# Two subtractions of the filter on VectorE instead of GpSimd

## The chip, the core and the metric

The kernel runs on one core of one Trainium2 chip. A core has TensorE (PE, with its weight load PEld), VectorE (DVE), ScalarE (ACT), GpSimd (POOL) and SyncE (SP), which issues DMAs; each works through its own instructions in order. The metric is the device time of one execution in microseconds. Before the change: 3201.36 us, the median of 3 runs (3199.89 to 3202.30).

## The reference, cut to what matters

Three parts follow one another. The change lies in the first, a filter in the frequency domain over 4 batches of 3072 rows of 256 columns:

```python
X = np.fft.rfft(x, axis=1)
Yr = Xr @ w_r - Xi @ w_i + b_r
Yi = Xr @ w_i + Xi @ w_r + b_i
Yr = np.sign(Yr) * np.maximum(np.abs(Yr) - lam, 0.0)   # the same for Yi
y = np.fft.irfft(Yr + 1j * Yi, n=3072, axis=1)
```

The second part makes u and v from relu(y @ w_in), normalises v over its columns, mixes it over all 3072 rows with w_spatial, adds a bias, multiplies by u and by w_out. The third is relu(x @ w_in) squared, scaled, and multiplied by another w_out. All data are float32.

## The kernel before

Every product is made in split precision: an operand is written as a high part (a copy in a type of fewer bits, fp32r) and a low part (the operand minus the high part), and two or three matmuls of the parts are added in PSUM. So each operand that comes from memory needs a copy (high) and a subtraction (low) before TensorE can use it.

The filter is a Fourier transform in two factors, 3072 = 96 x 32, and back. Its pieces, by function:

- `s1`: 96-point transform of x; one call takes a tile of two columns of the 96 x 32 grid. 16 calls a batch. The result `ps_z` goes through `z_sb` to the scratch tensor `zd`.
- `g_stage`: 32-point transform of t (what `zd` holds, read in another order) into `ps_g`, of which there is one buffer (`pg` has one). It is evacuated as `xh` (ScalarE, L375, L376), `xt` and `xl` (VectorE, L379, L380) and a negated copy (ScalarE, L383).
- `mix`: the products with w_r and w_i into `ps_m`, then the threshold: `ma`, `mt` (VectorE, L424, L425), `yh` (ScalarE, L426), `yl` (VectorE, L427).
- `g2_stage`: 32-point transform back into `ps_v`, evacuated by ScalarE (`v_sb`, L444) to the scratch tensor `vd`.
- `s3`: 96-point transform back of v (what `vd` holds) into `ps_y`, two buffers, each freed by a VectorE addition into `y_sb` (L469). Four calls make one chunk `y_hl` (L478, L482).
- `v_product`: of the second part, v = relu(y @ w_in) into `ps_vp`, its statistics (`bn`, `mv`) and, for three tiles at a time, a chain of small VectorE operations on 128 x 3 numbers (`rs`, L595 to L603) whose end releases the normalising L607 on ScalarE and L609 on VectorE.

The order of the work is written out by hand. The loop over k (L629 to L676) has 50 steps; each makes one `g_stage(k)`, one `mix(k - 1)`, one `g2_stage(k - 2)` and, spread over the step so that the counts come out, calls of `s1`, `s3` and `v_product`. The evacuations are not issued where their product is: each goes into a list of stages (`ch`), of which every further call issues one. After the loop a tail (L688 to L698) runs what is left of `s3` and `v_product`, while the first loads of the mixing are issued. x is done in the first 300 us; v is needed from about 144 us on.

`Stream` (L259) handles the three operands from memory: `xs` (tile `x_f`, both parts in one tile `x_hl`, 96 x 512), `ts` (`t_f`, `t_h`, `t_l`, 128 x 1024) and `vs` (`v_f`, `v_hi`, `v_lo`, 96 x 512). `load` issues the DMA, `make` the copy (L294, L296) and the subtraction (L298). `steady` is false until step k = 1, that is while the pipeline is filled; from then on the copies are ScalarE's. All three streams have `lo_on = "pool"`. GpSimd also issues the DMAs of the constants (`cg`, `cv`, L527) and of the normalised v (`vn`, L614).

Of the kernel before, what the change touches and what calls it, by code (L numbers as in the profile page):

```python
# [34 lines left out]
def f(ap):  # L35
    return ap.bitcast(F32)
# [191 lines left out]
def attention(tc, nc, x, w_r, w_i, b_r, b_i, c_f, c_b, c_g, c_v, c_s, zd, vd, yd, vn, chunks, cd, follow, nb=NB):  # L228
# [28 lines left out]
    steady = [False]  # L257

    class Stream:  # L259
# [25 lines left out]
        def make(self, n):  # L285
            while self.split < min(n, self.total):
                i = self.split
                self.load(i + 1)
                if self.loaded == i:
                    break  # L290
                raw = self.t[i]
                hi, lo = self.parts()
                if self.hi_on == "act" or steady[0] or i % 2 == 1:
                    nc.scalar.copy(hi, raw)  # L294
                else:
                    nc.vector.tensor_copy(hi, raw)  # L296
                on_pool = self.lo_on == "pool" and steady[0]
                (nc.gpsimd if on_pool else nc.vector).tensor_sub(lo, raw, f(hi))  # L298
                self.t[i] = (hi, lo)
                self.t.pop(i - self.bufs, None)  # L300
                self.split += 1
# [923 lines left out]
```

## Time and profile before

| | us |
|---|---|
| median of 3 timed runs | 3201.36 |
| the profiled execution, its own time | 3198.43 |
| its span in the trace | 3196.7 |
| TensorE busy (matmul) | 3085.7 (97%) |
| VectorE busy | 2309.5 (72%) |
| ScalarE busy | 1428.3 (45%) |
| GpSimd busy | 392.8 (12%) |

The filter takes the span up to about 556 us; the rest is the mixing and the output. Shares are of the whole span; the filter's own are in the rows below, by stretch. Busy time counts a stalled instruction as busy. Releasers of a wait are inferred. The granted clock is TensorE's, as a share of full speed (1.00 is 2.4 GHz, 0.50 is 1.2 GHz).

### The profile page before, as it was taken

Reading aid. Unit: us, or ns where it says so; the run is one execution under the profiler, and the core shown is the slowest. Engines: PE = TensorE matmul, PEld = TensorE weight load, DVE = VectorE, ACT = ScalarE, POOL = GpSimd, SP = SyncE. Lnnn points to the kernel's source line nnn. Section 1 sums busy time; section 2 is a strip of 40 time slices with the busy share of each in tenths; the row PEclk is TensorE's granted clock in tenths of the full one; section 3 lists DMA queues with packets and bytes.
Section 4 is the critical chain, followed back from the end, with each engine's and each line's share of the span. In section 5 each row is a group of like instructions: output and inputs, shape, how many; then the busy total and the mean of one; then the engine's idle time right before and its main releaser. Section 6 shows DMA issues by size and latency. Waiting matters only on the chain.

```text
span 3196.7 us, 46508 instructions
## 1 busy us (share of the span) xinstructions
PE 3085.7 (97%) x17960; PEld 3012.8 (94%) x17960; DVE 2309.5 (72%) x3495; ACT 1428.3 (45%) x2244; POOL 392.8 (12%) x497
## 2 busy tenths in 40 slices
PE   6989998999999999999999999999999999999999
PEld 5888986999999999999999989999999999999999
DVE  5877988787878888888878755656566656656564
ACT  5776766433434333434434334444444444444443
POOL 2665544021000210000000100000000000000000
PEclk7999999999999999999999999999999999999999
DMA  8987659487456956466471621111111111110210
GB/s 245 291 263 228 228 184 322 162 314 288 159 198 200 359 212 233 148 217 246 158 238 44 239 82 55 48 50 65 55 65 55 65 55 65 55 64 29 70 45 15
DMA packets 230517, 488.30 MB, mean 153 GB/s; under 512 B 22356, under 2 KB 116376, under 8 KB 230296
## 3 DMA queue, kind: packets, MB, share of 16 engines
q1 hardware_dynamic: 197224, 353.51, 33.4%
q0 software_dynamic: 33072, 131.82, 11.2%
q8 instruction: 140, 2.29, 0.3%
q14 instruction: 81, 0.66, 0.1%
HBM read 322.72 MB, written 162.53 MB: 152 GB/s over the span
## 4 chain that ended last, share of the span: by engine, by line
PE 76%; DVE 13%; DMA 5%; ACT 3%; issue 2%; POOL 0%; SPq 0%; ACTq 0%; DVEq 0%; POOLq 0%
PE acc L856 28%; PE ps_h L1066 17%; PE oacc L1087 17%; PE ps_o L1047 4%; PE ps_u L1029 4%; PE ps_m L413 3%; PE ps_vp L578 2%; DMA st_a<-in_moe_w_spatial_dram 2%; DVE a_hl L837 1%; DVE kept L873 1%; DMA st_b<-vn 1%; DVE b_hl L837 1%; DMA st_b<-t 1%; PE ps_g L366 1%; DVE bn L591 1%
## 5 line engine op out<-in xcount | busy, mean ns | idle before, releaser
L856 PE MATMUL acc<-a_hl,b_hl 128*128 128x384 f32 x7056 | 1239.5, 336 | 32.7 <-DVE kept L873 13.3
L856 PEld LDWEIGHTS acc<-a_hl,b_hl 128*128 128x128 f32 x7056 | 1232.9, 189 | 39.3 <-ACT kept L877 13.0
L1066 PE MATMUL ps_h<-x_hl,w 128*128 128x384 f32 x3072 | 580.8, 337 | 1.5 <-ACT x_hl L1050 0.9
L1087 PE MATMUL oacc<-q_hl,w 128*128 128x384 f32 x3072 | 575.4, 336 | 0.6 <-DVE q_hl L1073 0.6
L1066 PEld LDWEIGHTS ps_h<-x_hl,w 128*128 128x128 f32 x3072 | 543.3, 188 | 2.1 <-ACT x_hl L1050 1.3
L1087 PEld LDWEIGHTS oacc<-q_hl,w 128*128 128x128 f32 x3072 | 537.0, 188 | 0.9 <-DVE q_hl L1073 0.8
L833 ACT CAST a_hl<-a 128x768 fp32r<-128x768 f32 x253 | 211.7, 837 | 524.1 <-PE acc L856 436.7
L1073 DVE TENSOR_TENSOR q_hl<-r,q_hl 128x768 fp32r<-128x768 f32 x256 | 245.4, 959 | 230.7 <-ACT q_hl L1072 230.7
L1071 DVE TENSOR_TENSOR r<-r 128x768 f32<-128x768 f32 x256 | 244.8, 956 | 204.4 <-ACT r L1070 204.4
L1072 ACT CAST q_hl<-r 128x768 fp32r<-128x768 f32 x256 | 213.7, 835 | 301.8 <-DVE r L1071 301.8
L1070 ACT ACTIVATE r<-ps_h 128x768 f32<-128x768 f32 x256 | 208.3, 814 | 310.6 <-PE ps_h L1066 307.2
L837 DVE TENSOR_TENSOR a_hl<-a,a_hl 128x768 fp32r<-128x768 f32 x253 | 241.4, 954 | 137.5 <-ACT a_hl L833 137.0
L837 DVE TENSOR_TENSOR b_hl<-b,b_hl 128x512 fp32r<-128x512 f32 x295 | 202.0, 685 | 0.0
L833 ACT CAST b_hl<-b 128x512 fp32r<-128x512 f32 x295 | 181.8, 616 | 0.0
L578 PE MATMUL ps_vp<-win,y_hl 128*128 128x512 f32 x576 | 154.5, 404 | 18.3 <-ACT v_sb L444 15.0
L874 POOL DMA_DIRECT2D md<-kept x112 | 60.7, 542 | 828.4 <-DVE kept L873 824.0
L1029 PE MATMUL ps_u<-y_hl,w 128*128 128x384 f32 x768 | 145.7, 339 | 1.8 <-DVE y_hl L1015 1.8
L1047 PE MATMUL ps_o<-g,w 128*128 128x384 f32 x768 | 139.2, 337 | 1.6 <-DVE g L1037 1.0
L578 PEld LDWEIGHTS ps_vp<-win,y_hl 128*128 128x128 f32 x576 | 102.1, 190 | 40.4 <-ACT v_sb L444 16.8
L1029 PEld LDWEIGHTS ps_u<-y_hl,w 128*128 128x128 f32 x768 | 135.5, 190 | 3.1 <-DVE y_hl L1015 2.1
L1047 PEld LDWEIGHTS ps_o<-g,w 128*128 128x128 f32 x768 | 133.4, 188 | 2.6 <-DVE g L1037 1.6
L873 DVE TENSOR_TENSOR kept<-acc,kept 128x768 f32<-128x768 f32 x112 | 102.9, 952 | 22.1 <-PE acc L856 21.1
(139 smaller groups left out, 3700.7 us busy)
## 6 DMA issues: line engine op xcount, KB each, us to landing
a<-in_moe_w_spatial_dram SPq DMA_DIRECT2D x144, 384.0 KB, 5.0
b<-vn SPq DMA_DIRECT2D x168, 256.0 KB, 5.3
md<-kept POOLq DMA_DIRECT2D x112, 384.0 KB, 5.3
m<-md SPq DMA_DIRECT2D x56, 768.0 KB, 5.6
st_a<-in_moe_w_spatial_dram SPq DMA_DIRECT2D x72, 384.0 KB, 6.4
vn<-vr POOLq DMA_DIRECT2D x96, 256.0 KB, 4.0
s<-a POOLq DMA_DIRECT2D x48, 384.0 KB, 5.8
x_f<-in_x_dram SPq DMA_DIRECT2D x32, 384.0 KB, 6.5
```

What stands on the lines that cost most here:

```text
L578: nc.tensor.matmul(ps, y[:, a, k, o:o + 128], win[k][:, w, :], start=c == 0, stop=c == 5)
L833: nc.scalar.copy(s[:, 0, :], t)
L837: sub(s[:, 1, :], term.pop((kind, n)), f(s)[:, 0, :])
L856: nc.tensor.matmul(acc[d][:, h, 0:TH], b[:, m, d * 128:(d + 1) * 128], a[:, w, h * TH:(h + 1) * TH], start=fresh and i == 0 and c == 0, st ...
L1029: nc.tensor.matmul(ps[:, d, 0:TH], win[k][:, a, o:o + 128], y[:, w, k, :], start=c == 0, stop=c == 5)
L1047: nc.tensor.matmul(ps[:, h, 0:TH], wo[k // 2][:, a, o:o + 128], g[:, w, k, :], start=c == 0, stop=c == 11)
L1066: nc.tensor.matmul(ps[:, e, 0:TH], w[:, a, o:o + 128], x[:, i, j, :], start=c == 0, stop=c == 5)
L1070: nc.scalar.activation(r, ps[:, :, 0:TH], AF.Relu)
L1071: nc.vector.tensor_mul(r, r, r)
L1072: nc.scalar.copy(s[:, 0], r)
L1073: nc.vector.tensor_sub(s[:, 1], r, f(s)[:, 0])
L1087: nc.tensor.matmul(ps[:, h, 0:TH], w[:, a, o:o + 128], s[:, i, e, :], start=ff == 0 and c == 0, stop=ff == 2 * NP - 1 and c == 2)
```

## The change

One condition in `Stream.make`: GpSimd is chosen for the subtraction only if the stream is the one of t.

```diff
                 else:
                     nc.vector.tensor_copy(hi, raw)
-                on_pool = self.lo_on == "pool" and steady[0]
+                on_pool = self.lo_on == "pool" and steady[0] and self.tag == "t"
                 (nc.gpsimd if on_pool else nc.vector).tensor_sub(lo, raw, f(hi))
```

The subtractions of x and v go to VectorE's queue at the place where `make` is called. On VectorE, in a step of the loop in which two tiles of x are made and none of v (the first stretch), before the change:

```order
L424 TENSOR_SCALAR ma<-ps_m 128x512
L425 TENSOR_TENSOR mt<-ps_m,ma 128x512
L427 TENSOR_TENSOR yl<-mt,yh 128x512
L379 TENSOR_TENSOR xt<-ps_g,xh 128x512
L380 TENSOR_TENSOR xl<-ps_g,xt 128x4x128
```

On VectorE, the same step with the change:

```order
L424 TENSOR_SCALAR ma<-ps_m 128x512
L425 TENSOR_TENSOR mt<-ps_m,ma 128x512
L298 TENSOR_TENSOR x_hl<-x_f,x_hl 96x512
L427 TENSOR_TENSOR yl<-mt,yh 128x512
L298 TENSOR_TENSOR x_hl<-x_f,x_hl 96x512
L379 TENSOR_TENSOR xt<-ps_g,xh 128x512
L380 TENSOR_TENSOR xl<-ps_g,xt 128x4x128
```

One subtraction has come between `mt` and `yl`, one between `yl` and `xt`. In steps with one tile of x only the second is there. On VectorE, later, at the start of the third batch (both x and v are made), the difference at one place where two tiles of v are made:

```order
 L391 MEMSET x_2824 128x2
 L595 TENSOR_SCALAR rs<-mv 128x3
+L298 TENSOR_TENSOR v_lo<-v_f,v_hi 96x512 x2
 L482 TENSOR_TENSOR y_hl<-y_sb,y_hl 128x768
 L469 TENSOR_TENSOR y_sb<-ps_y,y_t 128x2x96
```

Two subtractions have come between the first operation of an `rs` chain and the low part of `y_hl`; the rest of the chain follows behind the `y_sb` addition. On GpSimd, in steps of the loop in which v is made, what stands there with the change:

```order
L614 DMA vn_69<-vr 128x512 x3
L527 DMA cg<-in_c_g_dram 128x1024
L527 DMA cv<-in_c_v_dram 128x1024
L298 TENSOR_TENSOR t_l<-t_f,t_h 128x1024
L614 DMA vn_69<-vr 128x512 x3
L527 DMA cg<-in_c_g_dram 128x1024
L527 DMA cv<-in_c_v_dram 128x1024
```

The subtractions of x and v that stood between these rows are gone from GpSimd; one of t in every second step stays.

## Rows read from the trace of the kernel before

**Rows 1.** Table of stretches: start:end, length; busy of each engine (instructions); clock, DMA.

```profile
56.00:144.00 88.00, 85.79 (x652) 80.80 (x651) 70.31 (x116) 62.27 (x127) 51.64 (x42) 1.00 0.89 282
144.00:291.00 147.00, 136.25 (x917) 123.73 (x918) 115.28 (x242) 105.57 (x230) 90.57 (x86) 0.98 0.78 249
291.00:470.00 179.00, 169.66 (x1182) 156.56 (x1181) 160.04 (x374) 120.19 (x263) 84.86 (x87) 0.99 0.64 207
470.00:546.00 76.00, 62.35 (x326) 48.80 (x325) 65.73 (x194) 50.76 (x115) 35.59 (x42) 0.98 0.97 338
```

**Rows 2.** The same stretches, GpSimd alone: v_lo subtractions, then x_hl subtractions.

```profile
144.00:291.00 147.00, 27.20 (x20) 0.98 0.78 249
291.00:470.00 179.00, 35.61 (x26) 0.99 0.64 207
470.00:546.00 76.00, 22.97 (x18) 0.98 0.97 338
...
56.00:144.00 88.00, 27.83 (x21) 1.00 0.89 282
144.00:291.00 147.00, 25.94 (x20) 0.98 0.78 249
```

**Rows 3.** Line 298: shortest/median/longest ns, first and last start; idle before it (us, times).

```profile
L298 POOL TENSOR_TENSOR v_lo<-v_f,v_hi x64: 1275/1292/2099, 144.4 to 545.7; 96x512 fp32r<-96x512 f32 x64
L298 POOL TENSOR_TENSOR x_hl<-x_f,x_hl x41: 1260/1292/1762, 60.9 to 290.9; 96x512 fp32r<-96x512 f32 x41
L298 DVE TENSOR_TENSOR x_hl<-x_f,x_hl x23: 679/689/690, 5.8 to 52.6; 96x512 fp32r<-96x512 f32 x23
...
L298 POOL TENSOR_TENSOR t_l<-t_f,t_h x22: 2394/2406/2437, 64.5 to 425.0; 128x1024 fp32r<-128x1024 f32 x22
...
  ACT v_hi L294: 104.7, 34
```

**Rows 4.** Timeline, VectorE: start, duration, instruction, [idle before, releaser]; three stuck operations.

```profile
61.35 1.37 DVE L427 TENSOR_TENSOR yl<-mt,yh 128x512 fp32r<-128x512 f32 x1 [0.92 <-ACT yh L426]
...
425.00 2.40 DVE L601 SCALAR_TENSOR_TENSOR rs<-rs 128x3 f32<-128x3 f32 x1
...
541.17 1.01 DVE L595 TENSOR_SCALAR rs<-mv 128x3 f32<-128x3 f32 x1
```

**Rows 5.** Timeline of 197 to 202 us, four engines; last, the stretch behind it.

```profile
197.28 1.29 POOL L298 TENSOR_TENSOR x_hl<-x_f,x_hl 96x512 fp32r<-96x512 f32 x1
197.38 1.21 DVE L601 SCALAR_TENSOR_TENSOR rs<-rs 128x3 f32<-128x3 f32 x1
199.02 0.17 DVE L601 SCALAR_TENSOR_TENSOR rs<-rs 128x3 f32<-128x3 f32 x1
199.62 0.81 ACT L607 ACTIVATE vr<-vr,rs 128x512 f32<-128x512 f32 x1 [2.46 <-DVE rs L603]
201.69 0.50 PE L578 MATMUL ps_vp<-win,y_hl 128*128 128x512 f32 x1 [2.44 <-ACT v_sb L444]
...
203.00:206.00 3.00, 3.00 (x14) 2.88 (x13) 1.97 (x5) 2.45 (x5) 1.97 (x2) 0.50 1.03 329
```

**Rows 6.** Timeline, a step of the first stretch: VectorE, ScalarE, the next ps_g matmul.

```profile
110.55 1.02 DVE L427 TENSOR_TENSOR yl<-mt,yh 128x512 fp32r<-128x512 f32 x1 [0.74 <-ACT yh L426]
...
111.81 0.69 DVE L379 TENSOR_TENSOR xt<-ps_g,xh 128x512 f32<-128x512 f32 x1 [0.24 <-ACT xh L376]
112.12 0.64 ACT L294 CAST x_hl<-x_f 96x512 fp32r<-96x512 f32 x1
112.53 0.69 DVE L380 TENSOR_TENSOR xl<-ps_g,xt 128x512 fp32r<-128x512 f32 x1
...
113.75 0.28 PE L366 MATMUL ps_g<-cg,t_h 128*128 128x256 f32 x1
```

**Rows 7.** Table of stretches: 20 us of the third stretch.

```profile
380.00:400.00 20.00, 19.05 (x132) 17.37 (x131) 18.57 (x48) 14.88 (x33) 9.05 (x10) 1.00 0.68 216
```

**Rows 8.** Timeline, VectorE in the tail: the longest gap of a period.

```profile
514.75 0.69 DVE L591 BATCH_NORM_STATS2 bn<-vr 128x6 f32<-128x512 f32 x1 [1.02 <-ACT vr L616]
```

## The prediction

> **What bounds the kernel now.** I read the page first, for the order of size: TensorE is busy almost throughout, GpSimd hardly at all. That whole-span share says nothing on a change that touches only the first sixth, so the second view is the table of stretches [rows 1]. I cut the filter in four: 56 to 144 us (first and middle transforms, x split, no v yet), 144 to 291 (x and v split), 291 to 470 (v only), 470 to 546 (the tail: last transform and v product). In the first three TensorE is busy 85.8 of 88, 136.3 of 147 and 169.7 of 179 us; VectorE follows with 70.3, 115.3 and 160.0. In the tail it is the other way: VectorE 65.7 of 76, TensorE 62.4. So VectorE has 17.7, 31.7, 19.0 and 10.3 us free, and part of that is the 0.04 us that lies between two operations in a row (111.81 + 0.69 ends at 112.50, the next starts at 112.53) [rows 6]. The engine that gets the work is the second bound of three stretches and the first of the last.
>
> The third view is the timeline at places where TensorE waits. At 201.69 it sat idle for 2.44 us before a v product; a half-clock stretch follows (granted clock 0.50 from 203 to 206) [rows 5]. Back from there: ScalarE's L607 waited 2.46 us for VectorE's rs chain, and in that chain an operation on 128x3 numbers took 1.21 us where the next one of its line took 0.17. It ended at 198.59, 0.02 us after GpSimd's x_hl subtraction (197.28 + 1.29) [rows 5]. So what GpSimd does here holds VectorE up. That is the part of the change that can pay.
>
> **The change, part by part.**
> *Removed from GpSimd:* 64 v_lo and 41 x_hl of 1292 ns in the median, 136 us of its work [rows 3]. GpSimd sits idle for ScalarE's hi copies before these subtractions (104.7 us for v_hi alone [rows 3]), so the freed time is worth nothing directly. What is left on its queue is t_l, the cg/cv loads and the vn stores, all of which can only start earlier.
>
> *Added to VectorE:* the same 105 subtractions. The trace has that very form on VectorE in the fill: 689 ns [rows 3]; with the 0.04 us between neighbours 0.73. By stretch, from the counts [rows 2]: 21 x = 15.3 us; 20 x and 20 v = 29.2; 26 v = 19.0; 18 v = 13.1. Together 76.6 us.
>
> *Stalls that go:* reading the timeline of VectorE beside that of GpSimd from 56 to 546 us, 51 VectorE operations run over 0.1 us longer than others of their line, and end when a GpSimd subtraction ends. 35 of them stand behind an x_hl or v_lo, 27.6 us in all; the first is yl at 61.35 (1.37 us, behind an x_hl), the last rs at 541.17 (1.01 us, behind a v_lo) [rows 4]. By stretch 3.7, 8.7, 8.0 and 7.2 us. The other 16, 21.4 us, stand behind t_l, like the rs operation of 2.40 us at 425.00 [rows 4], where the last t_l starts [rows 3]. They stay.
>
> The Trainium skill ("SBUF — State Buffer", section "Who interferes with whom") says that VectorE and GpSimd share one port pair under an exclusive lock, which a VectorE instruction with two SBUF inputs needs, and that whichever starts first keeps the other out to its end. The trace agrees, by the stuck operations above. The rule also speaks against the change: each new subtraction has two SBUF inputs, so it can stand behind t_l itself.
>
> *New stalls:* 22 t_l of 2.4 us lie between 64 and 427 us, that is 53 of 363 us, 15% [rows 3]. Of the 87 new operations of that time, 15% would meet one, for half of it: 13 x 1.2 = 16 us as the upper end. The lower end is zero, since an operation that would have been stuck behind the same t_l anyway comes out at the same time. I take 6 us, nearer to zero, because 16 of the 22 t_l hold something up already.
>
> *Net load of VectorE by stretch* (added less stalls gone): +11.6, +20.5, +11.0, +5.9, in free time of 17.7, 31.7, 19.0, 10.3. Everywhere it fits by the sum, with 6.1, 11.2, 8.0 and 4.4 us left, or 3 to 8%, before the 6 us of new stalls. VectorE works in order and waits for ScalarE and TensorE in turn, so I don't expect it to run at 95% without making them wait. I go stretch by stretch.
>
> 56 to 144 us: the order puts an x subtraction between yl and xt in every step. It waits for ScalarE's x_hl copy (112.12 + 0.64), and then takes 0.73; so xt starts at 113.5 instead of 111.81, and xl, which frees the only ps_g buffer, ends 1.7 us later than 113.22. TensorE's next ps_g matmul came at 113.75, a slack of 0.5 [rows 6]: 1.2 us lost in such a step. In every second step yl is late behind t_l already, so the subtraction finds its input made, costs 0.7 and loses nothing against the slack. The other added x in a step, in front of yl, falls into the gap in which VectorE waits for yh (0.74 us at 110.55 [rows 6]), and is free. Mean 0.6 us over 14 steps, 8 us; but a TensorE that was late once has that much slack in the next step, so I take half: +4. Ends: -3.7 (stalls gone, rest hidden) and +11.6.
>
> 144 to 291: 11.2 us stay free, steps are longer (9 us and more), and the rs chains lose stalls of which one led to the 2.44 us wait and the half clock (3 us of work at 0.50, 1.5 us lost). Against it the order puts two v_lo in front of y_hl and rs, where they wait for two ScalarE copies. +3, ends -9 and +20.5.
>
> 291 to 470: the dense part has VectorE at 18.57 of 20 us [rows 7]. Per 20 us come 2.9 v_lo (26 in 179), 2.1 us, less 0.9 of stalls: +1.2 on 1.4 us free, which the 0.04 us gaps alone use up. Here each v_lo stands ahead of the y_sb addition that gives TensorE a ps_y buffer. Two thirds of the net load show: +7, ends 0 and +11.0.
>
> 470 to 546: the tail repeats every 16 us with four v_lo, 2.9 us, less two rs stalls (0.84 us as at 541.17, and one of half of that [rows 4]), 1.3: +1.6 on a VectorE whose only real gap in a period is 1.02 us [rows 8], part of which takes it up. About +1 in 4.75 periods: +4.5, ends 0 and +5.9.
>
> Later stages issue the same instructions; TensorE is busy there from 566 us on, and a later start is a later end. Sum: 4 + 3 + 7 + 4.5 = 18.5 us. The profiled execution took 3198.43 us, so 3216.9; it lies 2.9 us under the median of the timed runs (3201.36), which makes 3219.8, and I say 3219.
>
> **Rivals.**
> *Faster: the stalls were the price, and VectorE had room.* For it: the 2.44 us wait of TensorE hangs on a stall that goes, and the added load is smaller than the free time in all four stretches. It decides if VectorE's idle time lies in the same steps as the new work. Then the net load is hidden, and three such TensorE waits with their half clock (2.4 + 1.5 each, 12 us) shrink to little: about -10, 3191. Against it: the dense part has no room.
> The Trainium skill ("GPSIMD Engine Reference", section "4.1 Engine selection") gives two-input elementwise work to VectorE as about twice as fast. The rows agree on the ratio (1292 to 689 ns [rows 3]). By that rule the change saves 63 us of engine time; that makes no time on the path, since GpSimd had it free.
>
> *Much slower: VectorE becomes the bound throughout.* Then the whole net load shows, 76.6 - 27.6 = 49: 3250. For it: in-order VectorE feeds every buffer release. Against it: by the sums 6 to 11 us stay free in each of the first three stretches, and there TensorE, not VectorE, fills the step [rows 1].
>
> *No change:* gains at the rs chains pay for the delays elsewhere, 3201. That the subtractions stay on GpSimd is ruled out by the order.
>
> **Chances.** Forecast (about +7 to +35) 0.58; VectorE the bound throughout 0.12; no change 0.18; faster 0.12. A measurement of this kernel tells about 0.2% (6.4 us) from no change. So slower 0.70, same 0.18, faster 0.12. The likeliest case alone has 3208 to 3236; the range goes to the middle of the outer rivals, 3192 to 3246.
>
> **What would show it.** Right: VectorE's busy share in the four stretches, as far as they go then, at about 89, 90, 92 and 89% (before plus net load, over the longer stretch; before 80, 78, 89 and 86), GpSimd's share down to t_l and DMA; no VectorE operation of the rs line over 1 us after 430 us; TensorE's waits for y_sb and xl grown; the last filter product some 15 to 20 us later. Wrong: TensorE's idle time in the filter under before's, or VectorE under 88% in 291 to 470 us, or new stalls behind t_l of more than 16 us.

## The result and the profile after

The changed kernel takes 3234.41 us in the median of four runs (3231.27 to 3236.14), the kernel before 3201.09 on the same chip (3199.89 to 3202.3). The ratio is 1.0103, with a 95% interval of 1.0085 to 1.012: 33 us slower, where the forecast said 18.5. The profiled execution spans 3233.6 us, before 3196.7; the rows below are of these two executions, 36.9 us apart.

Two rows of the table of stretches of the kernel after, cut at the same times as [rows 1] (start:end, length; busy of TensorE, its weight loads, VectorE, ScalarE, GpSimd; granted clock, DMA share, GB/s):

```profile
144.00:291.00 147.00, 126.93 (x827) 114.50 (x827) 117.12 (x254) 94.52 (x203) 33.49 (x38) 0.94 0.74 232
291.00:470.00 179.00, 164.63 (x1113) 150.21 (x1112) 156.08 (x362) 115.92 (x253) 50.10 (x60) 0.97 0.64 201
```

TensorE did 827 instructions from 144 to 291 us where it had done 917. VectorE looks hardly busier than in [rows 1]: 117.1 us against 115.3, 156.1 against 160.0. But the cuts hold different work by now, so the next rows are cut by work: at the first ps_g product of steps 2, 16, 31 and 47, and where TensorE goes on with the mixing after a wait of 5.2 us that both kernels have. Before:

```profile
59.50:144.00 84.50, 82.29 (x625) 77.47 (x623) 68.40 (x110) 61.16 (x124) 51.64 (x42) 1.00 0.93 294
144.00:296.00 152.00, 141.25 (x957) 128.55 (x958) 119.34 (x249) 110.03 (x238) 95.22 (x88) 0.98 0.78 251
296.00:446.20 150.20, 143.74 (x1005) 132.97 (x1004) 135.33 (x316) 101.19 (x222) 71.81 (x76) 0.99 0.67 216
446.20:566.07 119.87, 95.41 (x518) 76.55 (x516) 103.03 (x294) 78.40 (x172) 49.75 (x61) 0.98 0.76 265
```

After:

```profile
61.00:151.10 90.10, 84.59 (x624) 79.08 (x623) 70.18 (x131) 61.39 (x125) 24.10 (x20) 0.98 0.89 266
151.10:318.80 167.70, 146.39 (x958) 131.96 (x958) 133.68 (x288) 110.46 (x237) 40.18 (x46) 0.95 0.71 226
318.80:480.50 161.70, 148.52 (x1006) 135.92 (x1005) 142.22 (x337) 101.48 (x222) 42.58 (x53) 0.97 0.64 201
480.50:600.50 120.00, 95.17 (x518) 75.16 (x516) 107.91 (x317) 78.10 (x172) 21.46 (x39) 0.99 0.77 265
```

The counts of TensorE now agree row by row, and the lengths can be subtracted: +5.6, +15.7, +11.5 and +0.1 us. The fill ahead of them is 1.5 us longer and everything behind them 2.5; together 36.9. Most of the loss, 27.2 us, lies in the two stretches in which v is split while the loop runs. VectorE's busy share there is 80% and 88%, against 79% and 90% before: it is busy 21.2 us longer there, and the stretches have become longer by more.

What VectorE waited for, from 61 to 600 us of the kernel after (line waited at, releaser: us in all, times, longest):

```profile
DVE x_hl L298 <- ACT x_hl L294: 34.8, 34, 1.9
DVE v_lo L298 <- ACT v_hi L294: 17.2, 18, 2.3
DVE bn L591 <- ACT vr L616: 6.7, 16, 0.7
DVE xt L379 <- ACT xh L376: 3.9, 9, 0.8
```

And before, from 56 to 566 us:

```profile
DVE bn L591 <- ACT vr L616: 15.7, 22, 1.1
DVE ma L424 <- PE ps_m L415: 13.9, 20, 1.3
DVE yl L427 <- ACT yh L426: 11.1, 14, 1.2
DVE y_sb L469 <- ACT y_t L487: 11.0, 14, 2.0
DVE xt L379 <- ACT xh L376: 8.9, 19, 0.8
```

Two waits that VectorE did not have before are now its longest, 52.0 us: the new subtractions stand at the head of its queue until ScalarE has made the high part. Most of this stands in the place of older waits, which shrink (bn from 15.7 us to 6.7, xt from 8.9 to 3.9). But what stands behind a subtraction in the queue now comes late for TensorE, whose longest waits after are:

```profile
PE ps_y L461 <- DVE y_sb L469: 22.4, 36, 2.0
PE ps_vp L578 <- ACT v_sb L444: 22.4, 11, 3.3
PE ps_g L366 <- DVE xl L380: 7.3, 6, 2.1
```

The same three before:

```profile
PE ps_y L461 <- DVE y_sb L469: 17.1, 21, 1.5
PE ps_vp L578 <- ACT v_sb L444: 15.0, 8, 4.1
...
PE ps_g L366 <- DVE xl L380: 0.8, 1, 0.8
```

They grow by 5.3, 7.4 and 6.5 us. For the low parts of line 298 themselves TensorE waits next to nothing: no wait for x_hl or v_lo is over 1.0 us in all. How one such wait comes about is seen in the timeline of the kernel after (start, duration, instruction, [idle before, releaser]):

```profile
211.97 1.14 ACT L294 CAST v_hi<-v_f 96x512 fp32r<-96x512 f32 x2
212.63 1.29 DVE L298 TENSOR_TENSOR v_lo<-v_f,v_hi 96x512 fp32r<-96x512 f32 x2 [0.66 <-ACT v_hi L294]
213.84 0.95 DVE L482 TENSOR_TENSOR y_hl<-y_sb,y_hl 128x768 fp32r<-128x768 f32 x1
214.97 0.68 DVE L424 TENSOR_SCALAR ma<-ps_m 128x512 f32<-128x512 f32 x1
...
216.96 0.16 DVE L603 SCALAR_TENSOR_TENSOR rs<-mv,rs 128x3 f32<-128x3 f32 x1
217.15 0.81 ACT L607 ACTIVATE vr<-vr,rs 128x512 f32<-128x512 f32 x1 [2.94 <-DVE rs L603]
218.59 0.58 ACT L444 COPY v_sb<-ps_v 128x512 f32<-128x512 f32 x1
219.22 2.00 PE L578 MATMUL ps_vp<-win,y_hl 128*128 128x512 f32 x4 [3.19 <-ACT v_sb L444]
```

It is the chain of [rows 5] again, ahead of the same v product, the seventh: ScalarE's L607 waits for the rs chain, and TensorE for ScalarE. No rs operation of it is stuck now. The chain starts late instead, behind 0.66 us of waiting and 1.29 us of two subtractions, and TensorE waits 3.19 us where it had waited 2.44. After that the clock falls from 2.4 GHz towards 1.2, as in [rows 5] (table of stretches, 4 us):

```profile
219.00:223.00 4.00, 3.78 (x13) 3.20 (x14) 3.11 (x7) 3.02 (x8) 1.08 (x2) 0.57 1.03 364
```

Behind the fill there are four such half-clock places in the filter before, and nine after; each begins within 1.5 us after TensorE has waited 1.6 to 4.1 us, though a wait of 2.1 us at 157 us has none behind it. The mean clock of the second equal-work stretch falls from 0.98 to 0.95. Clock missing times length is 8.4 us there, against 3.0; by this estimate about 5 of its 15.7 us are the clock's.

### The profile page after: what moved, and what is told of

It is laid out like the page before. It is cut to its first block, busy times and chain, and to the rows that moved or that the text cites. A ratio compares the mean times of both kernels' runs of the same rounds, so it can differ in the third digit from the quotient of the medians.

```text
span 3233.6 us, 46462 instructions
## 1 busy us (share of the span) xinstructions
PE 3101.9 (96%) x17960; PEld 3024.9 (94%) x17960; DVE 2337.1 (72%) x3600; ACT 1428.4 (44%) x2244; POOL 253.2 (8%) x392
## 4 chain that ended last, share of the span: by engine, by line
PE 71%; DVE 15%; DMA 6%; ACT 5%; issue 3%; SPq 0%; POOL 0%; ACTq 0%; DVEq 0%; POOLq 0%
PE acc L856 27%; PE ps_h L1066 16%; PE oacc L1087 16%; PE ps_o L1047 4%; PE ps_u L1029 4%; DMA st_a<-in_moe_w_spatial_dram 1%; DVE a_hl L837 1%; DVE kept L873 1%; PE ps_vp L578 1%; DVE b_hl L837 1%; DVE v_lo L298 1%; DMA st_b<-t 1%; PE ps_m L413 1%; DMA st_b<-vn 1%; DMA c_w<-in_moe_w_in_dram 1%
## 5 line engine op out<-in xcount | busy, mean ns | idle before, releaser
L578 PE MATMUL ps_vp<-win,y_hl 128*128 128x512 f32 x576 | 157.9, 411 | 28.3 <-ACT v_sb L444 22.4
```

Source lines behind the costliest of these rows:

```text
L578: nc.tensor.matmul(ps, y[:, a, k, o:o + 128], win[k][:, w, :], start=c == 0, stop=c == 5)
```

## The experiments

Two causes could have made the change slower: the load (105 more operations on a VectorE that is busy 79 to 90% of the filter) or the wait at the head of its queue. Against both stands what was gained, the stalls that went. The first runs split the change by tensor. The kernel before was timed anew beside each group of runs, so its median differs a little.

**Only x on VectorE** (e1) and **only v on VectorE** (e2), each in the kernel before:

```diff
-on_pool = self.lo_on == "pool" and steady[0]
+on_pool = self.lo_on == "pool" and steady[0] and self.tag != "x"    # e1
+on_pool = self.lo_on == "pool" and steady[0] and self.tag != "v"    # e2
```

> Only the subtractions of x go to VectorE; those of v stay on GpSimd. Theory A (the wait): the change costs its 33 us because each subtraction stands at the head of VectorE's queue until ScalarE has made the high part; in the trace after, VectorE was idle 34.8 us for x's copies and 17.2 us for v's, so x carries two thirds: 3218 to 3228 us. Theory B (the load): 105 operations of 0.73 us on an engine close to its bound; x is 41 of them, so about 13 us: 3210 to 3217 us. In both the first 150 us and the stretch with x and v get longer, and nothing behind 320 us does.

> Only the subtractions of v go to VectorE; those of x stay on GpSimd. Theory A (the wait): a third of the cost, 3208 to 3214 us. Theory B (the load): 64 of 105 operations, about 20 us: 3218 to 3226 us. The first 150 us should be as before in both.

Measured: x alone 3204.87 us, ratio 1.002 (1.0011 to 1.003); v alone 3226.12, ratio 1.0083 (1.0068 to 1.0098); before 3198.91. The two parts add up to the whole (1.0103), and v carries four fifths of it. I had expected x to carry the greater part, because it has most of the waiting; e2 came out at the upper end of what the load alone was to give, and e1 under both theories, so this pair alone does not decide between them. But the length of a wait is no price. VectorE's wait in e1, and TensorE's longest waits:

```profile
DVE x_hl L298 <- ACT x_hl L294: 32.7, 33, 1.8
...
PE ps_y L461 <- DVE y_sb L469: 16.9, 22, 1.5
PE ps_vp L578 <- ACT v_sb L444: 14.6, 8, 3.2
PE ps_g L366 <- DVE xl L380: 7.3, 6, 2.1
```

And in e2:

```profile
DVE v_lo L298 <- ACT v_hi L294: 25.3, 23, 2.8
...
PE ps_vp L578 <- ACT v_sb L444: 23.5, 12, 3.2
PE ps_y L461 <- DVE y_sb L469: 23.5, 35, 2.4
```

With 32.7 us of waiting x makes the kernel 6 us slower, and with 25.3 us v makes it 27 slower; both figures hold the load and the stalls as well. x's subtractions make xl late (7.3 us against 0.8) and leave TensorE's other two waits as they were. v's leave xl alone (1.2 us) and lengthen the other two, from 17.1 and 15.0 us to 23.5 each: the two v_lo stand ahead of y_hl, ma and the whole rs chain, at whose end TensorE waits.

**The load without the wait** (e3), from the changed kernel: the subtraction takes the raw tile from itself, so it needs nothing of ScalarE. The low part of x and v is zero in it; TensorE does as many products as before, and e4 below computes everything.

```diff
+late = steady[0] and self.tag != "t"
-(nc.gpsimd if on_pool else nc.vector).tensor_sub(lo, raw, f(hi))
+(nc.gpsimd if on_pool else nc.vector).tensor_sub(lo, raw, raw if late else f(hi))
```

> As the change, but the subtraction of x and v takes raw minus raw, so the low part is zero and the operation, same size and same place in the queue, does not wait for ScalarE's copy. The load of VectorE is the changed kernel's, the wait is gone. Theory A: 3190 to 3208 us, with TensorE's waits for v_sb back to before's or under it. Theory B: 3222 to 3236 us, as the change. In between (3209 to 3221) both have a part, in proportion.

Measured: 3199.99 against 3198.91, ratio 1.0004 (0.9994 to 1.0013). All 105 operations are on VectorE, in the same places, and nothing is lost on balance. That the load alone makes the change slower has fallen. VectorE's longest wait from 56 to 566 us, and TensorE's:

```profile
DVE ma L425 <- PE ps_m L416: 11.2, 13, 2.5
...
PE ps_vp L579 <- ACT v_sb L445: 15.6, 10, 3.2
```

Both subtractions are gone from the list of VectorE's waits for ScalarE, and TensorE's wait at the v product, 22.4 us in the change, is back near the 15.0 of before. From step 2 to the last v product VectorE is busy 420.9 us and idle 79.4 before, 448.7 and 84.4 in the change, and 453.5 and 47.7 here. Without the wait the new work goes into idle time; with it, idle time is no less than before and the work comes on top. The second and third equal-work stretch:

```profile
142.30:292.40 150.10, 140.49 (x959) 128.36 (x958) 136.43 (x288) 111.08 (x238) 40.95 (x46) 0.98 0.80 253
292.40:449.70 157.30, 146.58 (x1005) 134.34 (x1004) 143.31 (x337) 101.18 (x222) 42.61 (x53) 0.98 0.65 206
```

Against before that is -1.9 and +7.1 us. So in the second stretch the load is paid for by the stalls, at a VectorE that is 91% busy, and in the third it costs about what I had put down.

**No subtraction at all** (e6), from the changed kernel: the high part stands in for the low part of x and v.

```diff
+if steady[0] and self.tag != "t":
+    lo = hi
+else:
     (nc.gpsimd if on_pool else nc.vector).tensor_sub(lo, raw, f(hi))
```

> No subtraction of x and v at all, on no engine, after the fill: the high part stands in for the low part in the products. It prices the stalls behind GpSimd's subtractions (before minus this) and the load (the run without the wait minus this). If the stalls that go are worth something by themselves: 3180 to 3192 us, that is 8 to 20 us under before, and the load costs as much again. If they lie beside other waits: 3194 to 3200 us, and the load is free too.

Measured: 3177.59 against 3196.78, ratio 0.9941 (0.9926 to 0.9955): 19 us under before, at the upper end of the 8 to 20 expected. The second and third stretch:

```profile
140.90:284.30 143.40, 138.53 (x959) 127.23 (x958) 105.69 (x248) 110.63 (x238) 40.22 (x46) 0.99 0.83 267
284.30:429.30 145.00, 142.26 (x1006) 132.40 (x1005) 129.15 (x316) 101.62 (x223) 42.61 (x53) 0.99 0.69 223
```

This gives the account of the change. What goes with GpSimd's subtractions (the stalls, and any low part that came late): -0.59%, some 19 us. The load of them on VectorE (e3 less e6): +0.63%, 20 us. The wait for ScalarE (the change less e3): +0.99%, 32 us. Their intervals put together leave some 5 to 7 us to either side of each. The three add up to the measured +33 because each is a difference of two of the runs; what tests the account are the next two.

**The subtraction issued later** (e4). If the wait is the cost, an order in which VectorE comes to the subtraction when its input is ready should keep the gain. This computes everything: the subtraction is put on a list, and issued at the next split of x, at the end of the step, or just ahead of the product that reads it.

```diff
+def settle(self, i=None):
+    while self.pending and (i is None or self.pending[0][0] <= i):
+        self.pending.pop(0)[1]()
...
-(nc.gpsimd if on_pool else nc.vector).tensor_sub(lo, raw, f(hi))
+if steady[0] and self.tag != "t":
+    if self.tag == "x":
+        self.settle()
+    self.pending.append((i, lambda lo=lo, raw=raw, hi=hi: nc.vector.tensor_sub(lo, raw, f(hi))))
+else:
+    (nc.gpsimd if on_pool else nc.vector).tensor_sub(lo, raw, f(hi))
...
+xs.settle(j)          # s1, behind xs.make(j + 1)
+vs.settle(j // 2)     # s3, behind vs.make(j // 2 + 1)
+vs.settle()           # end of a step, start of s3_more
```

> As the change, with the full computation, but each subtraction of x is issued one call later (at the next split of x) and each of v at the end of the step, when ScalarE's copy should be done. Theory A: VectorE's idle time before these subtractions falls from 52 to under 10 us and the time to 3190 to 3208 us, like the run without the wait. Theory B: 3222 to 3236 us. A third possibility: the x or v buffers are held longer, and loads come late: then SyncE's and ScalarE's waits for x_f or v_f grow.

Measured: 3192.94 against 3198.91, ratio 0.9983 (0.9974 to 0.9992): 0.2% faster than before. Behind the fill VectorE no longer waits for ScalarE at either subtraction. TensorE's waits from 56 to 566 us:

```profile
PE ps_z L350 <- DVE x_hl L306: 8.4, 5, 4.7
...
PE ps_vp L590 <- ACT v_sb L455: 3.9, 4, 1.1
```

The wait at the v product, 22.4 us in the change and 15.0 before, is 3.9. It is 15.6 in e3, which is some 7 us slower than e4 and also has all the load and none of the wait; so a subtraction ahead of the rs chain seems to cost something even when it need not wait. A new wait stands in the list, for an x tile that is now made too late.

**x later, v at once** (e5): the condition of e4 reads `self.tag == "x"`, and v's subtraction stays where the change has it.

> All subtractions of x and v on VectorE; those of x issued one call later, those of v at once as in the change. So only v's wait is left. By the runs so far v alone on VectorE cost 27 us and x alone 6 us. If v's wait is the main cost, as that says: 3214 to 3228 us. If the two waits only cost together (each late copy delays the other's): 3196 to 3208 us.

Measured: 3221.87 against 3196.78, ratio 1.0082 (1.0067 to 1.0097). With x issued later, nearly all of the loss remains; with v later too (e4) it is gone. So v's wait carries most of the 32 us, the same answer as e2 from the other side. The second stretch is not wholly clean for this, since TensorE waits 15.9 us for x_hl here and 8.4 in e4; the third, where x is no longer split, takes 162.9 us against 153.5 in e4.

**Mixed** (e7): e4, but v on GpSimd at once while the loop runs and no x is left to split. The reason was that in the third stretch e4 takes 153.5 us and before 150.2.

```diff
+if steady[0] and self.tag == "v" and s1_done[0] == 16 * nb and not tail[0]:
+    nc.gpsimd.tensor_sub(lo, raw, f(hi))
+elif steady[0] and self.tag != "t":
```

> As the deferred version, but while x is finished and the loop still runs (about 300 to 450 us) v's subtractions go to GpSimd, issued at once as before the change. In the deferred version that stretch was the only one longer than before (153.5 against 150.2 us). If the load of VectorE is what costs there: the stretch returns to about 150 us and the time to 3187 to 3191 us. If not: 3192 to 3196 us.

Measured: 3193.48 against 3196.78, ratio 0.9992 (0.9983 to 1.0001), and the third stretch stays at 153.2 us. The idea failed: with the rest of e4 in place, GpSimd is no better there than VectorE. Why is not shown.

**t later on VectorE as well** (e8), and **x settled at the end of the step too** (e9), as edits against e4:

```diff
-if steady[0] and self.tag != "t":
+if steady[0]:
...
+ts.settle(k // 2)     # g_stage
+ts.settle()           # end of a step
+xs.settle()           # end of a step, e9 alone
```

> As the deferred version, and the subtractions of t on VectorE too, issued at the end of their step; GpSimd has no arithmetic left. It removes the last stalls (17.5 us in the deferred version, all behind t_l) and adds 22 operations of 1.23 us, 27 us. If stalls and load weigh the same: 3194 to 3204 us. If a stall weighs more than load, since it falls on the operation that is in front: 3186 to 3192 us.

> The version with all subtractions deferred on VectorE, with x's issued at the end of a step at the latest (before, the last tile of x was left over until TensorE needed it: a wait of 4.5 us at 294 us in that run's trace, 7.4 us in all on x_hl). If that wait was on the path: 3184 to 3189 us, 0.3% under before. If the stretch is bound by VectorE anyway: 3189 to 3193 us, no change against the version before it.

Measured: e8 3190.00 against 3196.78, ratio 0.9978 (0.9968 to 0.9988), the lowest ratio of the versions that compute everything; e9 3192.30 against 3195.61, ratio 0.9985 (0.9976 to 0.9994). The intervals of e4, e8 and e9 overlap, so no order among them is shown; that e8 fell in the range named for stalls that weigh more than load does not show that they do. The late x tile that e9 was to bring earlier is still there, in e8 (7.4 us in all, the longest 4.5) as in e9:

```profile
PE ps_z L350 <- DVE x_hl L306: 7.3, 5, 4.5
```

The timeline of e9 shows why the edit did nothing:

```profile
282.43 0.63 ACT L299 CAST x_hl<-x_f 96x512 fp32r<-96x512 f32 x1
...
293.13 1.21 DVE L306 TENSOR_TENSOR t_l<-t_f,t_h 128x1024 fp32r<-128x1024 f32 x1
294.27 0.68 DVE L306 TENSOR_TENSOR x_hl<-x_f,x_hl 96x512 fp32r<-96x512 f32 x1
```

ScalarE's copy is done at 283.06, 11.2 us before the subtraction starts. VectorE comes to it late, because at the end of the step x is settled last, behind v_lo and t_l; in e8 it stands behind the same two. No run puts it first.

The lengths of the equal-work stretches of all kernels, worked out from the starts of those products in each timeline (us; the column before the last ends with the last v product):

| kernel | fill | to step 16 | to step 31 | to step 47 | to the last v product | rest |
|---|---|---|---|---|---|---|
| before | 59.5 | 84.5 | 152.0 | 150.2 | 113.6 | 2636.9 |
| after | 61.0 | 90.1 | 167.7 | 161.7 | 113.8 | 2639.4 |
| e1, x only | 59.0 | 89.1 | 154.5 | 150.3 | 113.5 | 2636.0 |
| e2, v only | 59.6 | 84.5 | 164.1 | 162.5 | 115.3 | 2639.1 |
| e3, no wait | 60.0 | 82.3 | 150.1 | 157.4 | 111.5 | 2636.9 |
| e6, no low part | 58.8 | 82.1 | 143.3 | 145.0 | 109.6 | 2637.5 |
| e4, later | 59.6 | 84.9 | 147.8 | 153.5 | 111.3 | 2635.8 |
| e5, x later | 60.1 | 84.9 | 159.7 | 162.9 | 113.8 | 2639.4 |
| e7, mixed | 59.8 | 85.0 | 144.8 | 153.2 | 111.5 | 2636.5 |
| e8, t too | 59.9 | 83.9 | 143.7 | 154.5 | 111.6 | 2636.8 |
| e9, x at the end of the step | 59.4 | 83.6 | 145.9 | 153.5 | 111.7 | 2630.9 |

The fill is the same program in e1 and in the change, and so is the stretch to step 16 but for its end; they differ by 2.0 and 1.0 us. The rest, the same in all kernels, differs by up to 8.5. So a difference of some 2 us in a stretch, or of several in the rest, can be scatter.

## Why the prediction was right in its sign and too small

The measured time lies in the stated range, and in that of the likeliest case; the forecast of +18.5 was little more than half of the measured +33. That the sign was right is in part luck. By its terms 11.5 of the 18.5 us were net load (the third stretch and the tail), and by e3 the net load comes to 1 us over the whole kernel. What made the kernel slower is the wait, 32 us, which the sum has only in the first two stretches, for 7.

- **First stretch, +4; measured +5.6.** The step held: x alone (e1) gives +4.6 there, v alone nothing. By e3 the load less the stalls is -2.2 there, and by the change less e3 the wait is +7.8. The 1.5 us in the fill can be scatter: e1, the same up to there, has -0.5. In the timeline after, an x subtraction waits, xl comes late, and so does ps_g, as worked out from [rows 6]:

```profile
97.43 0.69 DVE L298 TENSOR_TENSOR x_hl<-x_f,x_hl 96x512 fp32r<-96x512 f32 x1 [1.54 <-ACT x_hl L294]
...
99.70 0.40 PE L366 MATMUL ps_g<-cg,t_h 128*128 128x256 f32 x1 [1.97 <-DVE xl L380]
```

- **Second stretch, +3; measured +15.7.** This is the step that failed. The mechanism was named ("two v_lo in front of y_hl and rs, where they wait for two ScalarE copies") and then set off against the stalls at the rs chains, as though they were nearly of one size. By e3 the load less the stalls is -1.9 us here, and by the change less e3 the wait is +17.6. The free 11.2 us of VectorE were the wrong measure: the sum asked whether the work fits, and the time was lost because VectorE stood still with work behind it. The bound of +20.5 held, though it was made of net load.
- **Third stretch, +7; measured +11.5.** The net load was right in size (e3: +7.1). The wait adds 4.3 and was left out.
- **Tail, +4.5; measured +0.2.** The nine rs operations that were stuck there by 0.5 to 1.5 us, the last of them that at 541.17 in [rows 4], take 0.17 us each after, and the 18 subtractions, 5.9 us more than those stalls, did not lengthen it: by e3 the load less the stalls is -2.1 us here, and the wait +2.3, neither of them clear of scatter.
- **Later stages, 0; measured +2.5** in one profiled execution, which is within what the rest differs by among these runs. No run takes it apart.
- **New stalls behind t_l, 6 us (named, but no term of the sum); they did not come.** After, 16 VectorE operations are stuck behind t_l for 18.4 us, before 16 for 21.4. Six of them are now v_lo, the longest 1977 ns, but then others are not: the lower end, named in the prediction, was the right one. The rows of line 298 after:

```profile
L298 DVE TENSOR_TENSOR v_lo<-v_f,v_hi x64: 667/687/1977, 150.9 to 580.1; 96x512 fp32r<-96x512 f32 x64
L298 POOL TENSOR_TENSOR t_l<-t_f,t_h x22: 2363/2401/2494, 65.6 to 457.2; 128x1024 fp32r<-128x1024 f32 x22
```

- **The price of an operation** held: 687 ns, as the 689 of [rows 3]. The stalls that go were undercounted at 27.6 us: without the subtractions (e6) VectorE is 36 us less busy from step 2 to the last v product, 13.6 of them in the second stretch alone, where the count had 8.7. What the sum leaves free is 4 to 8% of each stretch, not 3 to 8.
- **The signs to look for.** VectorE was expected at 89, 90, 92 and 89%; by equal work it is 78, 80, 88 and 90%. The first three are short of it, since VectorE waited. In 291 to 470 us it is at 87% (156.08 of 179), which is one of the signs of being wrong; the other two did not come. The last filter product comes 34 us later, not 15 to 20. Two rs operations over 1 us remain after 430 us, since t_l now runs to 457 us; none comes behind that. TensorE's waits for y_sb and xl grew as said.
- **The rivals.** *Faster* took the gain for 10 us; it is about 19 (e6), and equals the load, so it does not come out alone. *VectorE the bound throughout* (3250) is as far off in time as the forecast (3219), and by the wrong road: e3 has all the load and is no slower. *No change* would have been right for the load and the stalls by themselves.

## What to carry to other kernels

When an operation is moved to a busy engine that works in order, price three things apart: its duration, the stalls that go, and the time in which it stands at the head of the queue with its input not made; here these were 20, -19 and 32 us. Look at what is queued behind it, not only at how long it waits: x, with 33 us of waiting, made the kernel 6 us slower, and v, with 25, made it 27 slower. Where the input comes late, issue the operation later, at a place in the order where its input is made and little waits behind it; here that turned 1.0% slower into 0.2% faster.

## What the runs showed of the hardware

GpSimd's 136 us of small subtractions, on an engine that was busy 12% of the time, cost the whole kernel about 19 us (e6, 0.9941). Part of that goes through the VectorE operations that they held up, and part may go through low parts that came late; no run parts the two. An operation on 128x3 numbers of 0.16 us can be held 2.2 us in this way (line 601 after, longest 2374 ns, behind a t_l). Where no subtraction is left on GpSimd (e8) no rs operation takes over 0.18 us. And lost time came with more lost time: half-clock places in the filter went from four to nine, each just behind a wait of TensorE, such as the one of 3.19 us that ends at 219.22.
